# Scores one place earlier in the order of a group: behind the first of seven products, from the third tile on

## The chip, the core and the metric

The kernel runs on one core of a Trainium2 chip. The metric is device time in microseconds (us) of one execution; less is better. The core has five engines with a queue each: TensorE (PE in the rows, its weight loads PEld), VectorE (DVE), ScalarE (ACT), GpSimd (POOL) and SyncE (SP), which issues all transfers here.

## The reference

A chunked attention is followed by two feed-forward networks, all in float32. There are 8 x 8 heads, 576 rows each, in chunks of 64.

```python
scores = scale * np.matmul(q_c, k_c.transpose(0, 1, 2, 4, 3))
scores = scores - np.max(scores, axis=-1, keepdims=True)
attn = np.exp(scores)
attn = attn / (np.sum(attn, axis=-1, keepdims=True) + 1e-09)
out = np.matmul(attn, v_c)
...
x = attn_out.transpose(0, 2, 1, 3).reshape(4608, 512)
h = x @ w_in             # 512 -> 2048
x = (h * np.cos(h)) @ w_out
a = x @ w1               # 512 -> 1024
b = x @ w2
out = ((a * b) @ w3) @ w_out2
```

## The kernel before, in words

The 4608 tokens are nine tiles of 512. Every float32 operand of a large product is split in a high and a low part, and a product is three matmuls (`mm3`, L103 to L107). The first network runs in two passes: the first takes 5 of 8 pairs of hidden blocks for each tile, the second the other 3. One pair of one tile is a **group**, numbered i. TensorE's work in a group is the product x @ w_in of this group, the product with w_out of the group before (`x2_mm`, in two halves "x" and "y"), and, in the first four groups of a tile of the first pass, one block of the attention of the next tile.

From the third tile on, x @ w_in is made by seven products of half size in place of eight (`Seven`, L454 to L501). `step1` makes the first (L474 copies its result, x1), `step2` the second and third, which VectorE adds to x1 (L482, the tile d), `step5` the fourth and fifth (L492, L494), `step3` the sixth and seventh (L501). Each step takes the next bank of a pool of two, so `step5` writes the bank that x1 was read from, and `step3` the bank that d was read from.

An attention block has five steps. `att_scores` (L348) makes 32 small matmuls into two banks, and on VectorE two maxima and two subtractions (L360, L362); `att_softmax` is the exponential (L368, ScalarE); `att_scale` sums and inverts on VectorE and multiplies on POOL (L377); `att_transpose` makes four transposes (L384) that ScalarE copies (L386); `att_values` makes 32 matmuls into two banks (L397) that ScalarE copies to xf (L402). Scores, transposes and values take their banks in turn from one pool of two:

```python
ps_at = ctx.enter_context(tc.tile_pool(name="ps_at", bufs=2, ...))
...
else ps_at.tile([P, HP, P], F32, tag="at", name=f"{name}{c}")
```

so that the two banks of a block's values are the two that the next block's scores write.

The order inside a group is written by hand, one string for each kind of group, and the loop at the end goes through it letter by letter; each engine gets its instructions in that order. The letters that matter here: `1`, `2`, `5`, `3` are the steps of the seven products; `q` is the next step of the attention block (the first `q` of a group is the scores, then softmax and scale, transposes, values); `s` splits the g of the group before (L563 on ScalarE, L564 on POOL); `x`, `y` are the halves of the w_out product; `b`, `d` are Abs and Sin on ScalarE (L550, L551); `M`, `h`, `H` prepare weights; `B`, `D` are products on VectorE (L555). `ORDER1` holds for the groups 10 to 40 that aren't the last of their tile. Group 40 has no attention block, so 24 groups with scores go by it: the first to fourth of the tiles three to eight. The fifth group of a tile goes by `ORDER1E`, has no attention, and splits the x operands of the next tile (`o`, L100 and L101).

Of the kernel before, what the change touches and what calls it, by code (L numbers as in the profile page):

```python
# [37 lines left out]
ORDER0E = "PsvaAQvcCxybBodDoooL"  # L38
ORDER1P = "PsqMhQqqHaclAxqbCrRmBdyqDL"
ORDER1PE = "SPsQacATCoobBoxodoDyoo"  # L40
ORDER1 = "1s2qMh5qqHa3clAxqbCrRmBdyqDL"
ORDER1E = "S1s25a3cATCoobBoxodoDyoo"
ORDER2 = "1s2h5a3clAxbCrdByDm"
ORDER3 = "12sqhlrmq5a3cAbCdBDxy"
# [11 lines left out]
def chunk_attention_two_ffn(  # L56
# [634 lines left out]
    with tc.manual_schedule():  # L691
# [18 lines left out]
        def order_of(i, nth, end):  # L710
# [4 lines left out]
            if i <= iA:  # L715
                return ORDER1E if end else ORDER1
            if i < iB:
# [196 lines left out]
```

## Time and profile before

| what | value |
|---|---|
| time, median of 3 runs (lowest, highest) | 1530.96 us (1529.14, 1536.62) |
| time of the profiled execution | 1526.43 us |
| its span, first to last instruction | 1524.7 us |
| TensorE busy in the span | 1474.8 us, 97% |
| VectorE, ScalarE, POOL busy | 1107.7, 772.9, 265.2 us |

The profiled execution is one run of the program with the profiler on; the 1.7 us outside its span belong to its time. Busy time of TensorE is counted from pipelined matmuls, so that a matmul's own duration is longer than the distance to the next. Times in the rows count from the start of the span.

### The profile page before, as it was taken

The numbers are of one execution on the slowest core, as the hardware profiler recorded it, in microseconds if no ns is written. First come the engines' busy times: TensorE is split into PE (matmuls) and PEld (weight loads), VectorE is DVE, ScalarE is ACT, GpSimd is POOL, SyncE is SP. The second block draws the span as 40 slices with busy tenths as digits, with TensorE's granted clock in tenths as the row PEclk, the third lists the DMA queues.
The fourth block names the chain that finished last, engine by engine and source line by source line (L and its number), as shares of the span: only waits on it lengthen the run. The fifth ranks groups of instructions, "written<-read, shape, count | busy, mean of one in ns | idle before, by whom it ended". The sixth has DMA issues, their size and how long they took to land.

```text
span 1524.7 us, 28724 instructions
## 1 busy us (share of the span) xinstructions
PE 1474.8 (97%) x11340; PEld 1321.8 (87%) x11340; DVE 1107.7 (73%) x1876; ACT 772.9 (51%) x1349; POOL 265.2 (17%) x206
## 2 busy tenths in 40 slices
PE   5799999999999999999999999999999999999998
PEld 4788888888888889888888888999999999999998
DVE  6986788888888887867787877665655646656564
ACT  4777788888887875545555556221221212212121
POOL 0222222222222222221222222201101011010000
PEclk9899999999999999999999999999999999999999
DMA  7654556466664628988888875601101101011000
GB/s 246 211 187 151 203 174 216 151 242 204 205 219 128 242 72 317 360 323 313 292 298 318 278 275 193 256 8 49 56 1 56 36 21 57 1 56 56 1 28 28
DMA packets 103814, 248.82 MB, mean 163 GB/s; under 512 B 11520, under 2 KB 23552, under 8 KB 102016
## 3 DMA queue, kind: packets, MB, share of 16 engines
q1 hardware_dynamic: 103680, 246.99, 46.8%
q8 instruction: 90, 1.47, 0.4%
q14 instruction: 44, 0.36, 0.1%
HBM read 151.78 MB, written 95.16 MB: 162 GB/s over the span
## 4 chain that ended last, share of the span: by engine, by line
PE 70%; ACT 11%; DVE 10%; DMA 6%; issue 2%; POOL 1%; SPq 0%; ACTq 0%; DVEq 0%; POOLq 0%
PE acc L106 9%; PE acc L105 9%; PE acc L107 9%; PE ps_hh L105 9%; PE ps_hh L107 8%; PE ps_hh L106 8%; PE ps_aa L105 5%; PE ps_aa L106 5%; PE ps_aa L107 5%; ACT t L551 2%; ACT L368 2%; ACT L551 1%; ACT t L550 1%; POOL ex L377 1%; DVE ex L362 1%
## 5 line engine op out<-in xcount | busy, mean ns | idle before, releaser
L564 POOL TENSOR_TENSOR g<-t,g 128x512 fp32r<-128x512 f32 x144 | 199.6, 1408 | 585.2 <-ACT g L563 494.0
L100 ACT ACTIVATE phl<-e 128x512 fp32r<-128x512 f32 x72 | 45.5, 632 | 366.7 <-DVE e L662 358.6
L105 PE MATMUL acc<-g,w 128*128 128x512 f32 x576 | 228.0, 396 | 0.0
L106 PE MATMUL acc<-g,w 128*128 128x512 f32 x576 | 226.7, 394 | 0.1
L107 PE MATMUL acc<-g,w 128*128 128x512 f32 x576 | 224.8, 390 | 0.0
L105 PE MATMUL ps_hh<-T,w 128*128 128x256 f32 x680 | 197.8, 291 | 5.4 <-DMA T<-xs2T 3.2
L107 PE MATMUL ps_hh<-T,w 128*128 128x256 f32 x680 | 193.5, 284 | 2.3 <-DVE w L198 2.3
L106 PE MATMUL ps_hh<-T,w 128*128 128x256 f32 x680 | 193.3, 284 | 0.0
L482 DVE TENSOR_TENSOR d<-x,ps_hh 128x512 f32<-128x512 f32 x134 | 91.7, 685 | 129.3 <-PE ps_hh L107 100.3
L105 PE MATMUL ps_hh<-B,w 128*128 128x256 f32 x620 | 180.4, 291 | 4.8 <-DVE t L555 3.3
L106 PE MATMUL ps_hh<-B,w 128*128 128x256 f32 x620 | 177.0, 285 | 0.0
L107 PE MATMUL ps_hh<-B,w 128*128 128x256 f32 x620 | 176.8, 285 | 0.0
L105 PEld LDWEIGHTS ps_hh<-T,w 128*128 128x128 f32 x680 | 131.1, 193 | 10.8 <-issue 3.8
L107 PEld LDWEIGHTS ps_hh<-T,w 128*128 128x128 f32 x680 | 131.2, 193 | 2.8 <-DVE w L198 2.7
L106 PEld LDWEIGHTS ps_hh<-T,w 128*128 128x128 f32 x680 | 131.3, 193 | 0.7
L105 PEld LDWEIGHTS ps_hh<-B,w 128*128 128x128 f32 x620 | 120.2, 194 | 11.7 <-DVE t L555 3.8
L107 PEld LDWEIGHTS acc<-g,w 128*128 128x128 f32 x576 | 108.2, 188 | 23.0
L106 PEld LDWEIGHTS acc<-g,w 128*128 128x128 f32 x576 | 108.5, 188 | 22.3 <-POOL g L564 3.1
L105 PEld LDWEIGHTS acc<-g,w 128*128 128x128 f32 x576 | 108.5, 188 | 19.5
L106 PEld LDWEIGHTS ps_hh<-B,w 128*128 128x128 f32 x620 | 120.2, 194 | 3.9
L106 PE MATMUL ps_aa<-T,w 128*128 128x256 f32 x432 | 122.5, 284 | 0.4 <-DVE T L101 0.4
L107 PE MATMUL ps_aa<-T,w 128*128 128x256 f32 x432 | 122.4, 283 | 0.0
(139 smaller groups left out, 3609.1 us busy)
## 6 DMA issues: line engine op xcount, KB each, us to landing
w<-sd SPq DMA_DIRECT2D x63, 512.0 KB, 7.3
sd<-raw SPq DMA_DIRECT2D x104, 256.0 KB, 4.2
qk<-in_q_dram SPq DMA_DIRECT2D x36, 256.0 KB, 4.5
qk<-in_k_dram SPq DMA_DIRECT2D x36, 256.0 KB, 4.6
vt<-in_v_dram SPq DMA_DIRECT2D x72, 128.0 KB, 3.1
x2a<-x2o SPq DMA_DIRECT2D x36, 256.0 KB, 2.7
x2a<-x2a SPq DMA_DIRECT2D x36, 256.0 KB, 6.8
x2d<-x2a SPq DMA_DIRECT2D x36, 256.0 KB, 2.9
```

What stands on the lines that cost most here:

```text
L100: nc.scalar.activation(dst[:, 0], src, AF.Copy)
L105: nc.tensor.matmul(ps, a[0], b[0], start=first, stop=False)
L106: nc.tensor.matmul(ps, a[0], b[1], start=False, stop=False)
L107: nc.tensor.matmul(ps, a[1], b[0], start=False, stop=last)
L362: nc.vector.tensor_tensor(out=ex[:, :, c], in0=ps[c], op=ALU.subtract, in1=mx[:, :, c].unsqueeze(2).to_broadcast([P, HP, 64]))
L368: nc.scalar.activation(ex, ex, AF.Exp, scale=SCALE)
L377: (nc.vector if early else nc.gpsimd).tensor_tensor(out=ex, in0=ex, in1=rc.unsqueeze(2).to_broadcast([P, 2 * HP, 64]), op=ALU.mult)
L482: nc.vector.tensor_tensor(out=two(self.d), in0=self.x1.unsqueeze(1).to_broadcast([P, 2, 256]), in1=two(p26), op=ALU.add)
L550: nc.scalar.activation(t, t, AF.Abs)
L551: nc.scalar.activation(t, t, AF.Sin, scale=-TWO_PI, bias=half_pi)
L564: nc.gpsimd.tensor_tensor(out=lo, in0=r, in1=f32(hi), op=ALU.subtract)
```

## The change

One string of the order is changed: the first `q` of `ORDER1` moves from behind `2` to behind `1`, ahead of `s` and `2`.

```diff
-ORDER1 = "1s2qMh5qqHa3clAxqbCrRmBdyqDL"
+ORDER1 = "1qs2Mh5qqHa3clAxqbCrRmBdyqDL"
```

ScalarE, POOL and SyncE keep the same instructions in the same order. TensorE's order changes in 24 groups. This is the third group of the third tile, before: the names ending in B_166, B_167 and T_168 are the x operands of the first, second and third product, ps_s the score banks, and the brackets name the engines or queues that a row waits for.

```order
L106 MATMUL ps_hh<-T_168,w 128x256
L107 MATMUL ps_hh<-T_168,w 128x256
L354 MATMUL ps_s_2605<-qk 64x64 [waits DMAHW3_49,DMAHW2_49,Activation_49]
L354 MATMUL ps_s_2606<-qk 64x64 [waits Activation_49]
L354 MATMUL ps_s_2605<-qk 64x64
```

And the same scores after the change, with the last matmuls of the first product ahead of them:

```order
L106 MATMUL ps_hh<-B_166,w 128x256
L107 MATMUL ps_hh<-B_166,w 128x256
L354 MATMUL ps_s_2585<-qk 64x64 [waits DMAHW3_49,DMAHW2_49,Activation_49]
L354 MATMUL ps_s_2586<-qk 64x64 [waits Activation_49]
L354 MATMUL ps_s_2585<-qk 64x64
```

The 32 score matmuls with their two waits for ScalarE have moved ahead of the 12 matmuls of the second and third product.

On VectorE the maxima and subtractions move with them. This is the first group of the fourth tile, as a difference; the two L101 rows are the last x operands that the group before splits, L482 makes d.

```order
 L101 TENSOR_TENSOR B_171<-xf,B_171 128x512
 L101 TENSOR_TENSOR T_172<-xf,T_172 128x512
+L360 TENSOR_REDUCE mx<-ps_s_3047 128x4
+L360 TENSOR_REDUCE mx<-ps_s_3048 128x4
+L362 TENSOR_TENSOR ex<-ps_s_3047,mx 128x4x64
+L362 TENSOR_TENSOR ex<-ps_s_3048,mx 128x4x64
 L482 TENSOR_TENSOR d<-x_3045,ps_hh 128x512
-L360 TENSOR_REDUCE mx<-ps_s_3067 128x4
-L360 TENSOR_REDUCE mx<-ps_s_3068 128x4
-L362 TENSOR_TENSOR ex<-ps_s_3067,mx 128x4x64
-L362 TENSOR_TENSOR ex<-ps_s_3068,mx 128x4x64
 L492 TENSOR_TENSOR e<-d,ps_hh 128x512
```

The four rows have moved from behind d to ahead of it.

## Rows read from the trace of the kernel before

**Rows 1.** The page, first part: busy us, share of the span, instructions of each engine.

```profile
PE 1474.8 (97%) x11340; PEld 1321.8 (87%) x11340; DVE 1107.7 (73%) x1876; ACT 772.9 (51%) x1349; POOL 265.2 (17%) x206
```

**Rows 2.** Busy time, 180 to 560 us: length, PE, PEld, DVE, ACT, POOL, clock, transfers.

```profile
180.00:560.00 380.00, 374.36 (x3602) 319.77 (x3603) 331.09 (x612) 311.55 (x525) 106.72 (x84) 1.00 0.58 192
```

**Rows 3.** Timeline of TensorE, third group of the fifth tile: start, duration.

```profile
330.80 0.66 PE L384 MATMUL ps_at<-ident,ex 128*128 128x128 f32 x4 [0.18 <-POOL ex L377]
...
335.46 0.28 PE L107 MATMUL ps_hh<-B,w 128*128 128x256 f32 x1
...
336.89 0.28 PE L107 MATMUL ps_hh<-T,w 128*128 128x256 f32 x1
337.10 0.70 PE L354 MATMUL ps_s<-qk 64*64 64x64 f32 x32
337.72 0.39 PE L105 MATMUL ps_hh<-T,w 128*128 128x256 f32 x1
```

**Rows 4.** Timeline of ScalarE, the same stretch.

```profile
331.49 0.60 ACT L386 ACTIVATE pt<-ps_at 128x512 f32<-128x512 f32 x1
...
335.83 0.64 ACT L402 ACTIVATE xf<-ps_v 128x256 f32<-128x256 f32 x2
```

**Rows 5.** Timeline of TensorE and ScalarE, second group of the fifth tile.

```profile
322.09 0.28 PE L107 MATMUL ps_hh<-B,w 128*128 128x256 f32 x1
...
323.52 0.28 PE L107 MATMUL ps_hh<-T,w 128*128 128x256 f32 x1
323.86 0.96 PE L354 MATMUL ps_s<-qk 64*64 64x64 f32 x32
324.75 0.39 PE L105 MATMUL ps_hh<-T,w 128*128 128x256 f32 x1
...
323.42 0.66 ACT L402 ACTIVATE xf<-ps_v 128x256 f32<-128x256 f32 x2
```

**Rows 6.** Timeline of VectorE and TensorE, first group of the fifth tile.

```profile
312.10 0.68 DVE L482 TENSOR_TENSOR d<-x,ps_hh 128x512 f32<-128x512 f32 x1
312.70 0.75 DVE L360 TENSOR_REDUCE mx<-ps_s 128x4 f32<-128x256 f32 x2
...
314.02 0.67 DVE L492 TENSOR_TENSOR e<-d,ps_hh 128x512 f32<-128x512 f32 x1
...
312.91 0.31 PE L105 MATMUL ps_hh<-B,s 128*128 128x256 f32 x1
```

**Rows 7.** Waits of the weight loads, 180 to 545 us: total, times, longest.

```profile
PEld ps_at L384 <- POOL ex L377: 14.0, 23, 2.2
PEld ps_v L397 <- issue: 8.1, 23, 0.4
PEld acc L106 <- POOL g L564: 2.0, 10, 0.2
PEld ps_s L354 <- ACT xf L402: 1.5, 6, 0.3
```

**Rows 8.** Timeline of the weight loads, first group of the third tile.

```profile
189.60 0.42 PEld L384 LDWEIGHTS ps_at<-ident,ex 128*128 128x128 f32 x4 [1.02 <-POOL ex L377]
```

**Rows 9.** TensorE by single microseconds: length, busy, clock, transfers.

```profile
66.00:67.00 1.00, 0.07 (x1) 1.00 0.92 359
...
68.00:69.00 1.00, 1.00 (x36) 0.76 0.14 37
69.00:70.00 1.00, 1.00 (x15) 0.50 0.40 94
70.00:71.00 1.00, 1.00 (x7) 0.50 0.88 293
71.00:72.00 1.00, 1.00 (x7) 0.53 0.87 336
...
203.00:204.00 1.00, 0.00 (x0) 1.00 0.17 57
...
205.00:206.00 1.00, 1.00 (x7) 1.00 0.00 0
```

## Prediction

> **What bounds the kernel now.** I read the shares of the whole page first. TensorE is busy for 1474.8 of 1524.7 us [rows 1], so time is won or lost only where TensorE waits. Then I read the stretch that the change touches, the third to the eighth tile, 180 to 560 us: TensorE is busy 374.36 of its 380 us, VectorE 331.09 and ScalarE 311.55, with the clock at 1.00 [rows 2]. TensorE has almost no slack there, and the other two follow at its pace. A wait that is added to TensorE is added to the total; the most that could be won is what it idles, 5.6 us. The list of waits says where that is: its weight loads wait 14.0 us in 23 places for POOL's softmax scaling ahead of the transposes (L384), but about 0.35 us of each is there even where nothing is late (the value products, L397, show 8.1 us in 23 places put down to "issue"). And six times the scores already wait for ScalarE's copies of the previous block's values (L402), 1.5 us in all [rows 7]. That last row is the one to look at, for the change moves the scores towards it.
>
> **The change part by part.** It touches four groups of each of six tiles, 24 in all. The queues of ScalarE, POOL and SyncE keep their order, and with it every DMA. TensorE makes the same products in another order: a score block of 0.62 us changes places with the second and third product of 1.44 us. On VectorE two maxima and two subtractions now stand ahead of the addition that makes d (L482). No instruction is added or removed, so all cost is in waits: the scores against the banks that they write, d against the product that reuses its bank, and the transposes against the softmax.
>
> *The score banks, third and fourth group of a tile.* The pool of these banks has two, and the previous block's two value banks are the ones that the next scores write. Follow one group. The transposes run at 330.80, the values' products end, and the first product's last matmul starts at 335.46 [rows 3]. ScalarE starts on their copy at 331.49, goes through two rounds of Abs and Sin, and reaches the values' copies at 335.83, with no idle time noted ahead of them; they end at 335.83 + 0.64 = 336.47 [rows 4]. Today the scores start at 337.10, 0.21 after the start of the last matmul ahead of them (336.89), and find the banks just freed. After the change they could start at 335.46 + 0.21 = 335.67. Matmuls alternate between both banks, so the block needs the second copy, and about 0.05 us to be woken (an estimate: in rows 5 the first score follows the first half of the copies by that much): 336.52. TensorE idles 0.85 us. It can't fade with time: ScalarE's row starts from TensorE's own transposes, so a later TensorE makes the copies later by as much. There are 12 such groups: 12 x 0.85 = 10.2 us.
>
> *The score banks, second group of a tile.* Here ScalarE also copies the finished tile ahead of the values (L588), and the copies end at 323.42 + 0.66 = 324.08. The scores could start at 322.09 + 0.21 = 322.30 and will start at about 324.13: 1.83 us. Of that the kernel pays some already: scores at 323.86 instead of 323.52 + 0.21 = 323.73, and 0.89 us from there to the next product where 0.62 is usual, together 0.40 [rows 5, 3]. Net 1.43 us, six times: 8.6 us.
>
> *The bank of d, first group of a tile.* No values stand right ahead of it, so the score banks are free. But VectorE comes late out of the group before (it splits the last x operands): it reaches d only at 312.10, though the product was ready, and d ends at 312.78. The product that reuses the bank starts at 312.91 [rows 6], 0.13 us later: no margin. With maxima and subtractions ahead (312.70 to 314.02, so 1.32 us) d ends at 314.10 and that product starts 1.32 us later. Ahead of the next output product a wait of 0.2 us for POOL's low part of g falls away with it (2.0 us in 10 places, [rows 7]; I count five). This holds in five tiles: 5 x (1.32 - 0.2) = 5.6 us. In the third tile's first group the transposes wait 1.02 us anyway [rows 8], on VectorE's chain, which ends no earlier: nothing. In the other groups d stays within the 1.44 us of the product after it: nothing; were that cover gone, d's own 0.68 us would show.
>
> *What is won.* Scores reach the softmax earlier by TensorE's count, so the transposes' wait shrinks. Above the usual 0.35 us it is 14.0 - 23 x 0.35 = 5.95 us [rows 7]. The two large ones of the third tile, 1.02 us [rows 8] and the longest of the list, 2.2 [rows 7], hold 2.5 of that; VectorE there is behind with weight sums, and I count 0.85 us of it (the net 1.43 by which TensorE comes later, less some 0.55 by which d's wait for its product holds VectorE's chain back: an estimate). The other 3.4 us should go, since TensorE arrives at least as late as they are long. Together 4.3 us. Bounds: nothing, and 6.
>
> Sum: 10.2 + 8.6 + 5.6 - 4.3 = +20.1 us. Against the profiled execution's own 1526.43 us that is 1546.5; its time is 4.5 us under the median of the runs shown, 1530.96, on which the same sum gives **1551 us**, 1.3% slower. Bounds of the terms: the banks' 18.8 lies between 8.6 (ScalarE gains on TensorE in the third and fourth groups) and 21 (a release that takes 0.15 us longer), the bank of d between 0 and 6.6, the gain between 0 and 6: +3 to +28 with all at one end, +15 to +26 as I read it, 1546 to 1557.
>
> **The clock.** New idle places lie in a stretch where the clock never falls now. An idle stretch that took nearly all of 66 to 67 us (TensorE busy 0.07) was followed by a clock of 0.76, 0.50, 0.50 and 0.53 of full, the lower of its two levels, in the microseconds from 68 to 72: 0.24 + 0.5 + 0.5 + 0.47 = 1.7 us lost. One that filled 203 to 204 us left it at 1.00, as the microsecond from 205 shows [rows 9]. So 1.83 us in the second groups may or may not cost the clock; 0.85 us has no row that speaks for it. The Trainium skill, "TensorE: Matmul & The Clock Gate", section "A second HAM failure mode: psum-queue depth-cycling", tells of a kernel whose many short idle places around PSUM banks made the clock swing between its levels; by that rule the sum would be the rival's below. The rows at 203 us do not follow it, those at 68 us do, and I leave it out of the sum.
>
> **The rivals.**
> 1. *The clock falls too.* In all six second groups: 6 x 1.7 = 10 us more, 1561; in every stalled group of the 18 about 30 more, which I take for remote.
> 2. *ScalarE gains on TensorE.* If the longer cycle lets ScalarE finish early, only the second groups' banks and d cost: 8.6 + 5.6 - 4.3 = +10, 1541. For it: ScalarE idles 68 of 380 us [rows 2]. Against it: the chain between the transposes' copy and L402 is started by TensorE [rows 3, 4], so idle time ahead of it shortens nothing.
> 3. *Not slower.* The values' copies leave the banks in time everywhere, and only d and the transposes count: 5.6 - 4.3 to 5.6 - 6.0, so 1531 to 1532. It decides from the point where L402 ends 0.85 us earlier behind the transposes than now (336.47 against 330.80). For it only that the wait is inferred: a bank freed by something else than L402 would not be late. Against it: the six waits that name L402 in [rows 7], at places where the copies end 0.2 us behind the scores' start.
> 4. *Faster.* Neither bank is late and the transposes' wait goes: -6 us, 1525, 0.4%, still inside what a measurement of this kernel tells from no change (0.5%, about 7.7 us).
>
> **How the numbers follow.** Forecast 0.62, rival 1 0.16, rival 2 0.12, rival 3 0.07, rival 4 with anything better 0.03. The predicted time is the forecast's, 1551. The range reaches down to rival 2 with 3 us for the level of the runs (they spread 1529 to 1537), 1538, and up to rival 1 with the same, 1564. Slower by over 0.5%: all of the forecast and of rivals 1 and 2 but a little that ends under +7.7 us, 0.88; within 0.5%, 0.10; faster, 0.02.
>
> **What would show it.** In the changed profile, TensorE waits for L402 ahead of L354 in 18 places, 0.8 us in twelve and 1.8 in six, some 21 us in all where there are 1.5 now. Ahead of the sixth product (the one on the B22 operand) it waits 1.3 us for L482 in five tiles. The transposes' rows show 0.35 us each but for the third tile. The first groups' scores start 1.4 us earlier behind the first product, with no wait. If the waits for L402 are absent or under 0.3 us, the anchor of ScalarE's chain is wrong and with it most of the sum; if they are there and the total stays, TensorE had slack that these views don't show. A clock under 1.00 between 190 and 560 us is rival 1.

## The result, and the profile after

The changed kernel takes 1551.54 us (median of six runs, 1549.15 to 1554.6); the kernel before, run beside it, 1529.27. The ratio is 1.0139 with a 95% interval of 1.0123 to 1.0155: 22.3 us slower. The prediction said 1551 us, 20 slower. The sum came out right; two of its parts did not, in opposite directions, and the runs below tell them apart.

The page of the changed kernel, first part, answers to [rows 1]:

```profile
span 1549.6 us, 28722 instructions
PE 1480.0 (96%) x11340; PEld 1330.4 (86%) x11340; DVE 1107.0 (71%) x1876; ACT 773.9 (50%) x1349; POOL 264.5 (17%) x206
```

The busy time of the stretch that the change touches, now 180 to 585 us, answers to [rows 2] (length, PE, PEld, DVE, ACT, POOL, clock, transfers):

```profile
180.00:585.00 405.00, 382.94 (x3621) 332.04 (x3620) 334.22 (x614) 315.16 (x530) 106.48 (x84) 0.98 0.54 181
```

TensorE idles 405.00 - 382.94 = 22.1 us there where it idled 5.6, and the clock's mean is 0.98 where it was 1.00. The list of TensorE's waits over the whole span names the places:

```profile
PE ps_s L354 <- ACT xf L402: 14.9, 18, 1.5
PE ps_hh L105 <- DVE d L482: 5.5, 5, 1.1
```

The weight loads' list for 180 to 585 us answers to [rows 7]:

```profile
PEld ps_s L354 <- ACT xf L402: 18.5, 18, 1.7
PEld ps_v L397 <- issue: 8.5, 24, 0.4
PEld ps_hh L105 <- DVE d L482: 8.0, 12, 1.3
PEld ps_at L384 <- POOL ex L377: 2.0, 2, 1.3
PEld acc L106 <- POOL g L564: 1.2, 6, 0.2
```

Eighteen waits for L402 and five large ones for d, as forecast. But the transposes' wait for POOL has all but gone from the list, 2 entries where there were 23, and with it the 0.35 us each that the prediction took for unavoidable.

The third group, timeline of TensorE, to [rows 3], and of ScalarE, to [rows 4], here in the fourth tile:

```profile
277.34 0.28 PE L107 MATMUL ps_hh<-B,w 128*128 128x256 f32 x1
278.13 0.96 PE L354 MATMUL ps_s<-qk 64*64 64x64 f32 x32 [0.51 <-ACT xf L402]
...
277.71 0.64 ACT L402 ACTIVATE xf<-ps_v 128x256 f32<-128x256 f32 x2
```

The scores could start at 277.34 + 0.21 = 277.55. They start when the first copy ends, at 278.13, 0.58 us late, and their row is 0.96 long where it was 0.70, since the second bank comes with the second copy: 0.84 us. The first group of the fifth tile, VectorE and TensorE, answers to [rows 6]:

```profile
318.18 0.75 DVE L360 TENSOR_REDUCE mx<-ps_s 128x4 f32<-128x256 f32 x2
318.84 0.75 DVE L362 TENSOR_TENSOR ex<-ps_s,mx 128x256 f32<-128x256 f32 x2
319.51 0.68 DVE L482 TENSOR_TENSOR d<-x,ps_hh 128x512 f32<-128x512 f32 x1
...
318.85 0.28 PE L107 MATMUL ps_hh<-T,w 128*128 128x256 f32 x1
320.24 0.39 PE L105 MATMUL ps_hh<-B,s 128*128 128x256 f32 x1 [1.11 <-DVE d L482]
```

Now the second group of the fourth tile, its timeline (to [rows 5]):

```profile
261.44 0.28 PE L107 MATMUL ps_hh<-B,w 128*128 128x256 f32 x1
263.19 0.96 PE L354 MATMUL ps_s<-qk 64*64 64x64 f32 x32 [1.47 <-ACT xf L402]
```

and the scores at the same place of the sixth tile:

```profile
398.57 0.96 PE L354 MATMUL ps_s<-qk 64*64 64x64 f32 x32 [1.47 <-ACT xf L402]
```

TensorE by single microseconds (length, busy, clock, transfers), first in the fourth tile, then in the sixth:

```profile
262.00:263.00 1.00, 0.00 (x0) 1.00 0.00 0
263.00:264.00 1.00, 0.81 (x32) 1.00 0.79 295
264.00:265.00 1.00, 1.00 (x15) 0.69 1.03 383
265.00:266.00 1.00, 1.00 (x7) 0.50 1.06 340
266.00:267.00 1.00, 1.00 (x7) 0.50 0.90 261
267.00:268.00 1.00, 1.00 (x7) 0.61 0.96 226
...
397.00:398.00 1.00, 0.10 (x1) 1.00 0.00 0
398.00:399.00 1.00, 0.43 (x10) 1.00 0.39 143
399.00:400.00 1.00, 1.00 (x34) 1.00 1.05 391
400.00:401.00 1.00, 1.00 (x11) 1.00 1.01 367
```

The same wait of 1.47 us is followed by a fall of the granted clock to 0.50, the lower of its two levels, in one tile and by none in the other. Between 170 and 590 us the clock falls four times, behind the second groups' waits of the tiles four, five, seven and eight; in the kernel before it never falls there.

**A ruler for the runs.** Each block's value products (L397) stand at the same place in every order, so the start of each, minus its start in the profile of before, says how late TensorE is by then; the growth from one block to the next is what one group costs. From the first to the last of 25 blocks, in the changed kernel:

```profile
166.72 0.69 PE L397 MATMUL ps_v<-pt,vt 64*64 64x64 f32 x32
...
572.26 0.70 PE L397 MATMUL ps_v<-pt,vt 64*64 64x64 f32 x32
```

and in the kernel before:

```profile
166.06 0.69 PE L397 MATMUL ps_v<-pt,vt 64*64 64x64 f32 x32
...
549.30 0.70 PE L397 MATMUL ps_v<-pt,vt 64*64 64x64 f32 x32
```

(572.26 - 166.72) - (549.30 - 166.06) = 22.3 us, which is what the medians differ by. (The two profiled spans differ by 24.9 us; the other 2.6 lie ahead of the first of these blocks and behind the last, where the ruler does not reach.) By groups, added over the six tiles ("first" includes the tile's last group before it), for this kernel and those that follow:

| kernel | first | second | third | fourth | all, us |
|---|---|---|---|---|---|
| changed | 4.5 | 11.4 | 3.1 | 3.4 | 22.3 |
| first groups alone | 4.5 | 0.0 | 0.0 | 0.0 | 4.6 |
| second groups alone | 0.0 | 8.5 | -0.4 | 0.0 | 8.1 |
| third and fourth alone | 0.0 | 0.2 | 3.1 | 3.4 | 6.7 |
| changed, copies early | 13.9 | 1.3 | 0.5 | 0.3 | 16.1 |
| scores between products 2 and 3 | 4.7 | 1.9 | -1.2 | -0.8 | 4.6 |
| changed, maxima behind d | 0.0 | 13.5 | 9.8 | 9.9 | 33.2 |
| old order, copies early in first groups | 0.1 | 3.3 | 0.1 | 0.0 | 3.5 |
| mixed | 0.0 | 3.3 | -0.5 | -0.9 | 2.0 |
| third and fourth between products 2 and 3 | 0.0 | 0.1 | -0.3 | -0.8 | -1.1 |
| changed, once more | 4.5 | 10.8 | 3.1 | 3.4 | 21.8 |

Single steps of one kind of group agree within some 0.15 us between tiles, the third tile and the places where the clock falls apart, so a tenth of a microsecond per group can be read, where the medians of runs move by several.

### The profile page after: what moved, and what is told of

The parts are those of the page before. It is cut to its first block, busy times and chain, and to the rows that moved or that the text cites. A ratio compares the mean times of both kernels' runs of the same rounds, so it can differ in the third digit from the quotient of the medians.

```text
span 1549.6 us, 28722 instructions
## 1 busy us (share of the span) xinstructions
PE 1480.0 (96%) x11340; PEld 1330.4 (86%) x11340; DVE 1107.0 (71%) x1876; ACT 773.9 (50%) x1349; POOL 264.5 (17%) x206
## 4 chain that ended last, share of the span: by engine, by line
PE 78%; ACT 9%; DVE 6%; DMA 5%; issue 1%; SPq 1%; POOL 0%; DVEq 0%; ACTq 0%; POOLq 0%
PE ps_hh L105 11%; PE acc L106 10%; PE acc L105 10%; PE acc L107 10%; PE ps_hh L107 10%; PE ps_hh L106 10%; PE ps_aa L105 5%; PE ps_aa L106 5%; PE ps_aa L107 5%; ACT t L551 2%; ACT L551 2%; PE ps_s L354 2%; ACT t L550 2%; DMA sd<-raw 1%; PE ps_at L384 1%
## 5 line engine op out<-in xcount | busy, mean ns | idle before, releaser
L564 POOL TENSOR_TENSOR g<-t,g 128x512 fp32r<-128x512 f32 x144 | 199.3, 1405 | 596.7 <-ACT g L563 446.3
L482 DVE TENSOR_TENSOR d<-x,ps_hh 128x512 f32<-128x512 f32 x134 | 91.8, 685 | 132.5 <-PE ps_hh L107 112.1
L105 PEld LDWEIGHTS ps_hh<-T,w 128*128 128x128 f32 x680 | 134.0, 197 | 10.5 <-ACT raw L252 4.5
L107 PEld LDWEIGHTS ps_hh<-T,w 128*128 128x128 f32 x680 | 133.8, 197 | 5.1 <-DVE w L198 5.0
L106 PEld LDWEIGHTS ps_hh<-T,w 128*128 128x128 f32 x680 | 134.0, 197 | 0.6
```

The costliest lines, as they stand in the source:

```text
L105: nc.tensor.matmul(ps, a[0], b[0], start=first, stop=False)
L106: nc.tensor.matmul(ps, a[0], b[1], start=False, stop=False)
L107: nc.tensor.matmul(ps, a[1], b[0], start=False, stop=last)
L482: nc.vector.tensor_tensor(out=two(self.d), in0=self.x1.unsqueeze(1).to_broadcast([P, 2, 256]), in1=two(p26), op=ALU.add)
L564: nc.gpsimd.tensor_tensor(out=lo, in0=r, in1=f32(hi), op=ALU.subtract)
```

## The experiments

**One kind of group at a time.** Three kernels, each with the new order in one kind of group and the old in the others (with `nth` the group's number in its tile from 0):

```diff
+ORDER1N = "1qs2Mh5qqHa3clAxqbCrRmBdyqDL"
...
-                return ORDER1E if end else ORDER1
+                return ORDER1E if end else ORDER1N if nth == 0 else ORDER1
```

and `nth == 1`, `nth >= 2`. Their lines are numbered one higher.

> New order in the first group of each tile alone; the other groups keep the old one. Theory (d comes late for the bank that the sixth product needs, and nothing else is late here): TensorE waits for L482 about 1.1 us ahead of the sixth product in five tiles, no new wait for L402, the clock stays at 1.00 there; +4 to +5 us over the kernel before, about 1533.5. Rival A (one cause hands down: the late d puts the engines out of step and the waits of the later groups follow from it): waits for L402 as in the whole change, +15 to +22 us. Rival B (the parts don't add up, a wait here is taken back in the next groups): 0 to +2 us.

> New order in the second group of each tile alone. Theory (score banks are held until L402, behind the copies of the finished tile): six waits of 1.5 us for L402 with the scores' own row stretched to 0.96 us, net +1.1 us each, +5 to +6 us in all; where the clock falls behind one of these waits another 1.5 us each, so +5.5 to +14 us, about +11 if four of six fall as in the changed kernel. Rival A (handed down from the first groups): no change. Rival C (the clock is the main loss of the whole change and falls in these groups only by chance of where the third and fourth groups put TensorE): clock at 1.00 and +5 us.

> New order in the third and fourth group of each tile alone. Theory: twelve waits of 0.5 us for L402 and rows of 0.96 us, 0.84 us lost each, some 0.3 us of it won back at the transposes; +6 to +7 us, about 1535.5, clock at 1.00. Rival A: no change. Rival B: under +3 us, the rest taken back.

Measured: 1534.95, 1538.49 and 1537.79 us against 1531.25; ratios 1.0022 (1.0004 to 1.0041), 1.0056 (1.0037 to 1.0075), 1.0036 (1.0021 to 1.0052). TensorE's waits, 170 to 590 us, one line of each kernel in that order:

```profile
PE ps_hh L106 <- DVE d L483: 5.5, 5, 1.1
```
```profile
PE ps_s L355 <- ACT xf L403: 9.0, 6, 1.5
```
```profile
PE ps_s L355 <- ACT xf L403: 6.1, 12, 0.5
```

Each kind of group has its own wait and its own cost, with next to nothing in the other columns of the table: nothing is handed down from the first groups (rival A), and little is taken back (rival B), at most the 0.4 us of the third groups behind late second ones. The costs of first, third and fourth groups are those of the whole change to 0.1 us. The second groups cost 1.1 us in three tiles, 2.6 in two and nothing in the third tile; the clock falls to 0.50 in just the two tiles that pay 2.6, so rival C, a clock of 1.00, is out. In the whole change four tiles paid 2.6, which is the difference of 3 us between 8.5 and 11.4.

**The copies out of the banks earlier.** TensorE's and VectorE's rows keep their order; ScalarE copies the values ahead of the second Abs and Sin.

```diff
-ORDER1 = "1qs2Mh5qqHa3clAxqbCrRmBdyqDL"
+ORDER1 = "1qs2Mh5qqHa3clAxqbCrRmByqdDL"
```

> The whole change, and the values' step stands ahead of the second Abs and Sin in the string, so that ScalarE copies the values out of the banks (L402) about 1.3 us earlier in its row; TensorE's and VectorE's order is that of the changed kernel. Theory (the banks are the loss): no wait for L402 in the third and fourth groups, some 0.5 us in place of 1.5 in the second, the clock at 1.00, the transposes' gain of 0.3 us per group kept, the first groups' wait for d kept: about the time of the kernel before, 1527 to 1533. Rival D (what delays the scores is not the copies but their place as such, or the load of qk): waits stay with another name, 1545 to 1552. Rival E (the later second Sin delays VectorE's last product and with it maxima and d): the waits for L402 go and waits for L482 come in all groups, 1540 or more.

Measured 1549.51 us, ratio 1.0108 (1.0084 to 1.0133): not the time of the kernel before. TensorE's waits, 170 to 590 us:

```profile
PE ps_hh L105 <- DVE d L482: 17.4, 17, 1.7
...
PE ps_s L354 <- ACT xf L402: 1.2, 6, 0.2
```

What was asked of the banks came true: the waits for L402 go from 14.9 us to 1.2, the third and fourth groups cost 0.1 us and less in place of 0.5, the second 0.2 in place of 1.1 or 2.6. But rival E came true as well: the weight loads wait for d in all groups, though for 0.3 us only in the third and fourth, and the 0.3 us that these were to win at the transposes does not show. The later second Sin delays VectorE's last product (L555), and with it d. Most of that falls where the expectation had not placed it, in the last group of a tile, whose row on VectorE is this (three of its rows, with d last):

```profile
307.78 0.69 DVE L555 TENSOR_TENSOR t<-t,e 128x512 f32<-128x512 f32 x1 [1.48 <-ACT t L551]
...
309.11 1.65 DVE L435 TENSOR_TENSOR spare<-xf,spare 128x512 f32<-128x512 f32 x1
310.69 0.68 DVE L482 TENSOR_TENSOR d<-x,ps_hh 128x512 f32<-128x512 f32 x1
```

TensorE waits 1.65 us for this d and then 1.25 for that of the first group; that is the 13.9 in the table. The Sin is only part of it. Idle time ahead of L555 is 1.48 us where the changed kernel has 0.58, 0.9 more; the other 0.96 us come from L435, 1.65 us long here and 0.69 in the changed kernel. What differs is POOL. In the changed kernel, L435 and POOL's split of g:

```profile
306.07 0.69 DVE L435 TENSOR_TENSOR spare<-xf,spare 128x512 f32<-128x512 f32 x1
306.18 2.98 POOL L564 TENSOR_TENSOR g<-t,g 128x512 fp32r<-128x512 f32 x2 [7.17 <-ACT g L563]
```

and POOL in this one:

```profile
308.67 3.22 POOL L564 TENSOR_TENSOR g<-t,g 128x512 fp32r<-128x512 f32 x2 [7.46 <-ACT g L563]
```

L435 takes 0.69 us where it starts 0.1 us ahead of POOL's row and 1.65 where it starts 0.44 behind it, in six tiles of each kernel; in the one tile of the changed kernel where it starts behind POOL's row, by 0.17 us, it takes 1.67. No run moves the one against the other alone, so that POOL's row is the reason is not shown.

**Scores between the second and third product.** `step2` is split in two letters, so that the score block has 0.72 us more of product behind the values than in the changed kernel.

```diff
-ORDER1 = "1qs2Mh5qqHa3clAxqbCrRmBdyqDL"
+ORDER1 = "16qs7Mh5qqHa3clAxqbCrRmBdyqDL"
...
+        def step6(self):
+            self.p26 = self.banks[1]()
+            self.prod(self.p26[:, H0], self.w[0], 1, "B21")
+        def step7(self):
+            self.prod(self.p26[:, H1], self.w[2], 0, "T2")
...
```

> Scores between the second and the third product in all four groups, so 0.72 us of product more between the values and the scores than in the changed kernel; VectorE's maxima still ahead of d. Theory (the loss is the time by which the copies out of the banks end too late): waits for L402 of about 1.1 us in the second groups and 0.1 in the third and fourth, clock at 1.00; net +0.4 us in the second groups, -0.1 to +0.1 in the third and fourth, +0.95 in five first groups for d as in the changed kernel; +5 to +7 us, about 1537. Rival D (the place behind one product as such, whatever the copies do): half the change's loss or more, +11 us. Rival A2 (d, once late, is late here too and costs more, since the third product ends later behind the scores): waits for L482 in all groups, +10 us or more.

Measured 1534.53 us, ratio 1.0029 (1.0012 to 1.0046); by the ruler +4.6. TensorE's waits (L494 is the d of L482 here):

```profile
PE ps_hh L105 <- DVE d L494: 5.4, 5, 1.1
PE ps_s L354 <- ACT xf L402: 4.5, 6, 0.8
```

The second groups wait 0.8 us where they waited 1.5, 0.7 less for 0.72 of product; the third and fourth have no wait left; no fall of the clock is seen (1.00 in the stretch). The loss follows the distance to the copies, not the place as such (rival D), and with five waits for d, as before, rival A2 is out too. And the third and fourth groups now win 0.1 to 0.3 us each.

**The maxima behind d.** TensorE as in the changed kernel, but the vector part of `att_scores` is called by a letter of its own, `Z`, behind `2`: `"1qs2ZMh5qqHa3cl..."`. The lines are shifted: L385 is the softmax scaling, L392 the transposes, L410 the copies.

> TensorE's order is that of the changed kernel, but VectorE's two maxima and two subtractions stay behind d, where they were; ScalarE and POOL as before. Theory (maxima ahead of d cost the first groups their bank, and give the transposes' gain in the others): no wait for L482 in the first groups, 0 there in place of 0.95; the same waits for L402 as in the changed kernel in the others, but the transposes wait for POOL again, since d and the maxima behind it come only after the third product: 1.5 us lost per third and fourth group in place of 0.5, 2 per second group (3.5 where the clock falls); +30 us or more, 1561 to 1570. Rival F (the gain at the transposes is only TensorE's own lateness, and the maxima's place does nothing for it): +12 to +18 us, 1543 to 1549, less than the changed kernel by the first groups' 5.

Measured 1565.17 us, ratio 1.0231 (1.0206 to 1.0256).

```profile
PE ps_at L392 <- POOL ex L385: 16.7, 18, 1.4
PE ps_s L354 <- ACT xf L410: 15.1, 18, 1.5
```

The first groups cost nothing now, so their 0.95 us was the maxima's place ahead of d. In the others the waits for L402 are the same, and the transposes wait for the softmax again: a third or fourth group costs 1.6 us in place of 0.5. (The clock fell in two of the six second groups here.) So what the changed kernel wins at the transposes is won by the earlier maxima, and rival F is out.

**Can both be had?** Three orders that take the good and leave the bad.

> The order of the kernel before, but in the first group of each tile the values' step stands ahead of the second Abs and Sin, so that the copies (L402) end earlier ahead of the second group's scores, the one place where the kernel before waits for them. Theory: those six waits go, 0.3 to 0.4 us each, and nothing else moves: -1.8 to -2.4 us, 0.12 to 0.16% faster. Rival E (the later Sin makes d late): waits for L482 in the second groups, 0 to +3 us.

> Each group by what the runs so far give: first group in the old order with the values' copies early at its end, second group in the old order, third and fourth with the scores between the second and third product. Theory: -1.8 to -2.4 us in the second groups as in the run with the old order, and -0.1 to +0.1 us in each of twelve groups; -1 to -3.5 us, at most 0.25% faster than the kernel before. Rival: the third and fourth groups cost 0.2 us each by a late d, and the sum is nothing.

> Scores between the second and third product in the third and fourth group of a tile alone; first and second group in the old order. Theory (parts add up, and these twelve groups won 0.10 to 0.28 us each where the whole run had them so): no wait for L402 and none for L482 that is new, the transposes' wait gone in these groups; -2.0 us between the same values' steps of the profile, 0.13% by the runs, which their spread may hide. Rival (the gain there was only the other groups' lateness): 0 to +1 us.

The first two (the copies early in the first groups, `ORDER1F = "1s2qMh5qqHa3clAxqbCrRmByqdDL"` where `nth == 0`; the second with the split order where `nth >= 2` besides) took 1534.77 us, 1.0021 (1.0005 to 1.0038), and 1531.83, 1.0012 (0.9997 to 1.0027), against 1531.51. The first missed its forecast, in sign too: the waits for L402 went, but the second groups got 0.34 us slower, 1.58 in the third tile. The weight loads' list, 180 to 585 us, says where to (L378 is L377):

```profile
PEld ps_at L385 <- POOL ex L378: 17.6, 24, 2.4
```

and in the kernel before, the same stretch:

```profile
PEld ps_at L384 <- POOL ex L377: 14.5, 24, 2.2
```

The transposes wait more, 17.6 us for 14.5: the later Sin makes the last product of VectorE late, then d, the maxima behind it, and the softmax. A wait was moved, not removed. In the third tile's second group the clock falls besides, behind a wait at the transposes and not for L402, which is the most of the 1.58:

```profile
211.41 0.66 PE L385 MATMUL ps_at<-ident,ex 128*128 128x128 f32 x4 [2.01 <-POOL ex L378]
...
213.00:214.00 1.00, 1.00 (x4) 0.50 0.04 14
```

The mixed kernel missed its forecast too: its second groups repeat the 3.3 us, the fall in the third tile included, against 1.4 won in the third and fourth, so +2.0 by the ruler where -1 to -3.5 was expected. The third kernel, with the split order where `nth >= 2` and the old order elsewhere, took 1529.53 us against 1530.53, ratio 0.9992 (0.998 to 1.0005): by the runs no difference, by the ruler 1.1 us won, half of what I had added up. The missing half lies in the third groups of the tiles four to six, which won 0.25 us each where all groups had the split order and 0.0 here. Why is open: that the second groups came late there is not enough, for in the mixed kernel they are 0.35 us late and the same third groups win nothing.

**The clock again.** The changed kernel, once more:

> The changed kernel once more, for its clock alone. Theory (the wait of 1.5 us in a second group lets the clock fall in some of the six and not in others, by where it happens to lie): the same waits for L402 to 0.05 us; second groups cost either 1.1 or 2.6 us, and which ones cost 2.6 is not the same set as before (tiles four, five, seven and eight). Rival (what falls is set by the program's own pattern of work): the same four tiles.

1550.61 us, a single run. These two waits are the same to the last digit:

```profile
PE ps_s L354 <- ACT xf L402: 14.9, 18, 1.5
PE ps_hh L105 <- DVE d L482: 5.5, 5, 1.1
```

The second groups cost 2.57, 1.07, 2.56, 2.57 and 1.09 us in tiles four to eight, where the first profile had 2.56, 2.56, 1.07, 2.58 and 2.58; the third tile's cost 0.98 where it had cost 0.03. The clock falls in just the tiles that pay more, this time three, four, six and seven; in the third:

```profile
197.00:198.00 1.00, 1.00 (x6) 0.50 1.05 358
```

So the set of tiles that pay for the clock changes from one execution to the next, with the wait the same. In the fourth to eighth tile a fall costs 1.5 us; in the third it costs 0.95.

## Why the prediction was right, and where it was not

**The score banks: right.** Expected 0.85 us for a third or fourth group and 1.83 for a second before what was already paid; measured 0.84, and for the second, from 261.44 + 0.21 = 261.65 to 263.19 with 0.27 more for the longer row, 1.81. That ScalarE's chain hangs on TensorE's own transposes, so that the wait can't fade, holds in all six tiles. The run with early copies and the one with scores between products show the cause from two sides, by the copies' time and by the scores'.

**The bank of d: right.** Forecast 1.32 us late in five tiles, and 0.2 given back; measured 320.24 - (318.85 + 0.12) = 1.27 late and 0.95 net. The run with the maxima behind d takes it to zero.

**What is won at the transposes: mis-sized.** The term read "14.0 - 23 x 0.35 = 5.95 us", of which 4.3 were counted. The 0.35 us, taken over from the value products' row, is no floor for the transposes: with the softmax in time their row in the list is gone but for two entries. With 0.84 us lost at the scores, the third and fourth groups cost 6.5 us, not 12 x 0.84 = 10.1: 3.6 won, 0.3 each. Where the clock held, the second groups of tiles four to eight cost 1.07 in place of 1.43, so another 0.3 to 0.4 each; and the third tile's second group costs next to nothing, its wait of 2.2 us at the transposes being cut to 0.8, by as much as it loses, where 0.85 us was counted for the whole tile. With the first groups, 4.8 net where 5.6 were counted, less 0.3 won in the third tile's (the 4.5 of the table), the parts come to 4.5 + 5.4 + 6.5 = 16.4 us without the clock where the sum had 20.1. Held against the losses (10.1 at the third and fourth groups' scores, 6 x 1.41 = 8.5 at the second ones', 4.8 at d), 7.0 us were won where 4.3 were counted, and more than the bound of 6.

**The clock: left out of the sum, and wrongly so.** Rival 1 had it at 1.7 us in each of six second groups and a chance of 0.16. It fell in four of six, at 1.5 us each by the ruler: 6 us; by the prediction's own sign, a clock under 1.00 in the stretch, rival 1 came true in part. The two errors, some 4 us too much and 6 too little, nearly cancel, and that is why 1551 was met: luck, as far as the sum goes. (On the kernel before as run beside it, 1529.27, the sum gives 1549.4.) The prediction read its two idle stretches of [rows 9] by single microseconds. The timeline of the kernel before has their lengths:

```profile
66.92 0.39 PE L107 MATMUL ps_hh<-T,w 128*128 128x256 f32 x1 [1.74 <-DVE w L198]
...
204.58 0.66 PE L384 MATMUL ps_at<-ident,ex 128*128 128x128 f32 x4 [1.79 <-POOL ex L377]
```

The shorter, 1.74 us, was followed by a fall and the longer, 1.79 us, by none, so these rows gave no reason for a term of nothing: something between 0 and 10 us belonged in the sum. The Trainium skill, "TensorE: Matmul & The Clock Gate", section "A second HAM failure mode: psum-queue depth-cycling", tells of frequent short idle places around PSUM banks that swing the clock. This trace agrees behind four of the six waits of 1.5 us. No fall followed the waits of 0.5 us in the kernel with the third and fourth groups alone, nor the five of 1.65 us for d in the run with early copies; the clock was 1.00 in both.

**The rivals.** That ScalarE gains on TensorE (2) and that the banks come free in time (3, 4) are out by the eighteen waits. What stays open: which of the second groups loses the clock. That it differs between executions is shown; what decides it is not, and the length of the wait alone does not.

## What to carry to other kernels

Before a consumer is moved up in a hand-written order, take the distance on each engine from the release of the bank it writes, not only from the data it reads: here the data was there, and 1.4 us of cover had hidden a copy that came 0.84 us after the new place. A queue in order passes such a shift on: the same four vector instructions won 0.3 us per group where they stood ahead of the softmax, and cost 0.95 where the next thing in the row was d. And a total that is met says little about its parts; a fixed landmark in each cycle, held against the same landmark of the kernel before, sized each kind of group to a tenth of a microsecond where medians of runs could not.

## What the runs showed of the hardware that I had not expected

A wait of TensorE of about 1.5 us, behind 0.7 us of product and ahead of the score block's small matmuls, was followed by a clock of 0.50 for some three microseconds in four of six places (1.5 us lost each time), and by 1.00 in the two others, in one execution; in another execution of the same program it was four of six again, at other places. In the kernel with the second groups alone, and in that with the maxima behind d, the same six waits were followed by two falls each. A weight load's wait that is put down to "issue" (0.35 us ahead of the value products, in every kernel here) is not a base that other loads share: ahead of the transposes it vanished. And a VectorE subtraction of two 128x512 operands (L435) took 0.69 us where it started 0.1 us ahead of POOL's rows (L564) and 1.65 where it started 0.44 us behind them.
